# Decayed attention and a two-layer MLP on one core: the prologue's weight steps, mask, first group of w_in and loads in another order

## The chip, the cores and the metric

The kernel runs on one core of one Trainium2 chip. The metric is the device time of one execution in microseconds (us), the median of the runs shown. The core's engines are TensorE (PE; PEld is its weight load), VectorE (DVE), ScalarE (ACT) and GpSimd (POOL); SyncE (SP) issues nearly all DMAs.

## The reference

Attention with a decayed state (batch 4, 8 heads, 768 positions, 64 channels, blocks of 64 positions), then an MLP on its 3072 tokens:

```
for b in range(nb):                      # 12 blocks of 64 positions
    intra = einsum('bhic,bhjc->bhij', qb, kb) * Dmask        # lam**(i-j), causal
    intra = einsum('bhij,bhjd->bhid', intra, vb)
    inter = einsum('bhid,bhde->bhie', qb * lam_pow, kv_state)
    out[:, :, sl] = intra + inter
    kv_state = lam_block * kv_state + einsum('bhsd,bhse->bhde', kb * rev_pow, vb)
h = x @ w_in                             # 3072x512 by 512x2048
g = maximum(h, 0)**2
return g @ w_out                         # 2048x512
```

## The kernel before

**Tiles.** Two blocks of 64 positions (a pair for all heads) are a chunk; chunks 0 to 3 give the tokens of the first group (m = 0, 512 tokens), chunks 4 to 7 those of the second. Every fp32 operand of the MLP is split into an upper part (fp32r, `wh`, `xh`, `gh`) and the rest (`wl`, `xl`, `gl`), and a product is the sum of three: upper by upper, rest by upper, upper by rest. So one column tile f of the hidden layer (`hidden(m, f)`, L638) is 12 products of 128x512, and its share of the output (`project(m, f)`, L674, L675, L679) 12 more.

**Order.** The program is laid out by hand: each engine runs its instructions in the order of the code, so an instruction that waits holds up all that stands behind it on its engine. The same holds for SP's loads.

**Prologue.** `warm(4)` (L79) multiplies zeros on PE. `get_near` makes from lam the near powers (ACT copy L384, DVE copy L385), `get_mask` the decay mask of a block (PE L391: 14 products of 64 by 32 columns; DVE copy L397 of 128x224), `get_qpow` the powers for q. Chunk t: `prep_k` and `prep_q` on POOL (L511, L506), `scores` on PE, `masked` on DVE (L517, the mask times the scores), `news` on PE (what the chunk adds to the states) and `state` on DVE (L546: the old state by the decay `fd`, plus the news, four instructions of 128x64 for each block), `early` on PE (the result), `split` (ACT L618 `xh`, DVE L619 `xl`). `copy_vx` and `copy_qx` (ACT L171, L176) copy halves of v and q to the other partitions.

**Weight units.** A unit u is a piece of both weights that is loaded by SP (`wload`, L227) and split by seven steps: ACT `first_hi` (absolute value, L244), DVE `clamp` (L257), ACT `first_lo` (L249), DVE `shift` (L261), `sign` (L268), `rounded` (L274), ACT `upper` (L285, into `wh`), DVE `lower` (L290, into `wl`). With `shared`, DVE does the first half of `lower` and POOL the second (L293), behind a marker copy of one element (L297, `turn`). Unit 0 is half as wide as the others (128x512 where they have 128x1024). Unit 0 feeds f = 0, unit u the column tiles behind it.

**Loads and gates.** A `gate` is a tiny ACT copy (L135) or DVE memset (L137) that writes into the buffer which a load is about to fill, so that the load waits for the engine's place in its order. In the prologue `gate(V, chunk 4)` stands behind `state(1)`, and `wload(2, nc.scalar)`, which has an ACT gate, behind the second `split`; SP issues unit 2 behind the first two loads of chunk 4.

**Group m = 0.** For f = 0 to 15 the loop runs `hidden(0, f)`, then for unit u = f + 2 the DVE steps `clamp`, `shift`, `sign`, the `upper` and `lower` of unit u - 1, then relu, square and rest of the tile (ACT L645, L649, L654, DVE L659 `gl`), `rounded`, and `project` of the tile before. Between them stand steps of chunks 4 to 7: `look` (scores and news), `masked`, `fade` (ACT L564: four instructions that multiply the state by the decay), `advance` (DVE L342: adds the news to it), `result` and `split`. At f = 0 and at f = 1 and 2 three extra products of 384 or 512 columns stand ahead of the 12 (L634); the first of the 12 writes over what they leave.

Behind m = 0 come a second group of the same kind (m = 1) and a part for the other 2048 tokens in a scheme with fewer products; the change touches neither.

Of the kernel before, what the change touches and what calls it, by code (L numbers as in the profile page):

```python
# [15 lines left out]
P = 128  # L16
B, H, S, D = 4, 8, 768, 64
C = 128
# [23 lines left out]
def body(ctx: ExitStack, tc: tile.TileContext, qT, kT, kvq, lam, w, out):  # L42
# [86 lines left out]
    def load_kf(t):  # L129
        nc.sync.dma_start(out=chunk[t]["kf"], in_=kT[t])  # L130
# [120 lines left out]
    def first(u):  # L251
        first_hi(u)
        first_lo(u)
# [81 lines left out]
    move = wk.tile([L, 2 * L - T], F32, name="move", tag="gh")  # L335
    nc.gpsimd.memset(move, 0.0)
    ones_where(move, L - T, [[-1, 2 * L - T]])
    mask = small.tile([P, 2, 2, L], F32, name="mask")


# [44 lines left out]
        V.tensor_copy(y[L:P], x)  # L385

    def get_mask():
        n = ps_h.tile([P, NB - 1, 4, T], F32, name="h")
        for b in range(NB - 1):
            for y, r in enumerate(rows):  # L390
                nc.tensor.matmul(  # L391
                    n[r, b], move[:, b * T : b * T + L], near[0:L, :, 2 * y : 2 * y + 2],
                    start=True, stop=True, skip_group_check=True,
                )
        for y, r in enumerate(rows):
            nc.scalar.copy(mask[r, :, :, L - T : L], near[r, :, 2 * y : 2 * y + 2])
        V.tensor_copy(mask.rearrange("k j a (b t) -> k b (j a) t", b=NB)[:, 0 : NB - 1], n)  # L397

    blk = wk.tile([H, NPR, L], F32, name="blk", tag="gh")
    nc.gpsimd.tensor_tensor(  # L400
# [7 lines left out]
    def get_qpow():  # L408
        q = two_banks(ps_a, "att")
        a, b = q[:, 0, 0 : NPR * L], q[:, 1, 0:4]  # L410
        nc.tensor.matmul(a, odd, blk.rearrange("h p i -> h (p i)"), start=True, stop=True)
        nc.tensor.matmul(b, half, four, start=True, stop=True)
        nc.scalar.copy(qpow.rearrange("k p i -> k (p i)"), a)
        nc.scalar.copy(fd, b)
# [34 lines left out]
                        )  # L449
        return g.begun  # L450

    def news(t, banks, at, begun=(), keys=range(2)):
# [3 lines left out]
        u_of[t] = [banks[1 - b][:, at : at + NPR * D] for b in range(n)]  # L456
        for a in range(2):
            for j in range(2):
                for y in range(2):
                    for b in range(n):  # L460
# [78 lines left out]
    def state(t):  # L539
        for b, u in enumerate(u_of.pop(t)):  # L540
# [11 lines left out]
            else:  # L552
                nc.scalar.copy(new, u)

    faded = {}

    def fade(t, b):
# [69 lines left out]

    g_of, accs = {}, {}

    def hidden(m, f, xh, xl):  # L630
# [206 lines left out]
    def early_news(t):  # L837
        second = ps_h.tile([P, DM], F32, name="h")
        news(t, [ps_h.tile([P, DM], F32, name="h"), second], 0)

    def first_scores(t, x):
# [6 lines left out]
    first(0)  # L848
    get_near()
    for op in (clamp, shift, sign, rounded):  # L850
        op(0)
    first_scores(0, banks())
    get_qpow()
    get_mask()
    prep_k(0)
    prep_q(0)
    prep_k(1)
    upper(0)
    copy_vx(0)
    masked(0)  # L860
    lower(0)
    early_news(0)
    state(0)
    first_hi(1)
    copy_qx(0)
    first_scores(1, banks())
    prep_q(1)
    copy_vx(1)
    masked(1)
    clamp(1)  # L870
    early_news(1)
    copy_qx(1)
    early(0, two_banks(ps_a, "att"))
    state(1)
    place(4)
    gate(V, chunk[4]["all"])
    first_scores(2, banks())
    low[0] = split(0, o[0])
    prep_k(2)
    prep_q(2)  # L880
    copy_vx(2)
    early_news(2)
    masked(2)
    first_lo(1)
    copy_qx(2)
    low[0]()
    load_part(4, 0)
    load_part(4, 2)
    early(1, banks())
    low[1] = split(1, o[1])  # L890
    wload(2, nc.scalar)
    load_kf(4)
    load_part(4, 1)
    load_vx(4)
    state(2)
    first_scores(3, two_banks(ps_a, "att"))
    place_rest(3)
    prep_k(3)
    prep_q(3)
    prep_k(4)  # L900
    prep_q(4)
    copy_vx(3)
    early_news(3)
    masked(3)
    low[1]()
    copy_qx(3)
    early(2, banks())
    low[2] = split(2, o[2])
    state(3)
    early(3, banks())  # L910
# [12 lines left out]
    lower(1, True)
    first_lo(2)
    opening.close()
# [1 line left out]

    prev = None
    for m in range(PLAIN):
        if m == 0:  # L930
            new_x(1)
        else:
            middle.close()
            ps_b = hidden_part.enter_context(tc.tile_pool(name="ps_b", bufs=1, side="right", space=PSUM))
            held += [
                wk.tile([P, KT, N], F32, name=f"held{k}", tag=n) for k, n in enumerate(("xh", "xl"))
            ]
        for f in range(NF):
            h = hidden(m, f, *xs_of[m])
            if m == 0:  # L940
# [16 lines left out]
                if u_ < NLOT:  # L957
                    if f:
                        clamp(u_)
                    if f == 1:  # L960
                        upper(u_ - 1)
                        lower(u_ - 1)
                    if f:
                        shift(u_)
                    sign(u_)
                if f > 1:
                    upper(u_ - 1)
# [22 lines left out]
                    copy_qx(t)  # L990
                if step == 2:
                    attend(t, o)
                if f == 0:
                    fade(t, 0)
                if u_ + 1 < NLOT:
                    first(u_ + 1)
                if prev is not None:
                    project(*prev)
                if step == 0:
                    look(t)  # L1000
                    if f:
                        fade(t, 0)
                if f >= NF - NPAIR:
                    w_plain(f - (NF - NPAIR))
            else:
# [495 lines left out]
```

## Time and profile before

| what | us |
|---|---|
| median of 3 runs | 566.7 (566.15 to 566.91) |
| the profiled execution | 566.81 |
| its span, first to last instruction | 565.0 |
| mean granted TensorE clock | 0.991 |

| engine | busy us | share of the span | instructions |
|---|---|---|---|
| PE | 555.0 | 98% | 5353 |
| PEld | 461.2 | 82% | 5353 |
| DVE | 438.2 | 78% | 763 |
| ACT | 348.3 | 62% | 617 |
| POOL | 83.0 | 15% | 96 |

All durations below come from the profiled execution, 0.11 us above the median; 1.81 us of its time lie outside its span. A timeline row gives an instruction's start, its duration, engine, line, operation, output and inputs, how many like it follow one another, and in brackets how long the engine was idle ahead of it and what ended the wait. A granted clock of 1.00 is 2.4 GHz, 0.50 is 1.2 GHz. One product on PE often has two records, and records of one engine overlap by some hundredths of a microsecond.

### The profile page before, as it was taken

How to read it: one execution, taken by the hardware profiler on the slowest of the kernel's cores; microseconds unless marked ns; L12 is line 12 of the kernel's file. 1: busy time of each engine (PE TensorE's matmuls, PEld its weight loads, DVE VectorE, ACT ScalarE, POOL GpSimd, SP SyncE). 2: the span in 40 equal slices, each digit the busy share in tenths (PEclk: the TensorE clock that was granted, in tenths of full speed). 3: DMA queues.
4: the chain of work that ended last, by engine and by line, in shares of the span. 5: the costliest groups of instructions: out<-in, count | busy, mean ns of one | idle time of the engine just before them, and what ended most of it. 6: DMA issues, size and time to landing. Idle time of an engine off the chain costs nothing.

```text
span 565.0 us, 13666 instructions
## 1 busy us (share of the span) xinstructions
PE 555.0 (98%) x5353; PEld 461.2 (82%) x5353; DVE 438.2 (78%) x763; ACT 348.3 (62%) x617; POOL 83.0 (15%) x96
## 2 busy tenths in 40 slices
PE   7899999999999999999999999999999999999997
PEld 4777888888888888887888878888888888888887
DVE  6889999967888755755655587877599889989884
ACT  2889988856666666664564687676754453443450
POOL 6523342341322223300000000000000000000000
PEclk8799999999999999999999999999999999999999
DMA  8577669976988865357899988999698999999541
GB/s 330 207 259 243 218 230 278 359 226 229 306 293 280 284 206 150 98 171 206 316 374 380 303 298 247 308 300 309 217 363 295 404 344 346 366 329 348 185 130 56
DMA packets 89407, 152.41 MB, mean 270 GB/s; under 512 B 7680, under 2 KB 34816, under 8 KB 89344
## 3 DMA queue, kind: packets, MB, share of 16 engines
q1 hardware_dynamic: 89344, 151.55, 80.0%
q8 instruction: 42, 0.69, 0.5%
q14 instruction: 21, 0.17, 0.1%
HBM read 113.77 MB, written 37.75 MB: 268 GB/s over the span
## 4 chain that ended last, share of the span: by engine, by line
PE 93%; DVE 3%; ACT 2%; issue 1%; POOL 0%; ACTq 0%; POOLq 0%
PE factor L1162 25%; PE h L815 18%; PE h L638 15%; PE acc L815 7%; PE acc L674 6%; PE acc L675 5%; PE acc L679 5%; PE h L428 4%; PE b L428 2%; PE att L428 2%; PE att L79 1%; PE h L1162 1%; ACT w L1306 1%; DVE w L1127 1%; DVE A L268 0%
## 5 line engine op out<-in xcount | busy, mean ns | idle before, releaser
L1162 PE MATMUL factor<-w 128*128 128x512 f32 (+1 forms) x614 | 109.4, 335 | 0.1
L1162 PEld LDWEIGHTS factor<-w 128*128 128x128 f32 x614 | 94.0, 188 | 13.7 <-DVE w L1127 0.6
L1125 ACT CAST w<-kept 128x1024 fp32r<-128x1024 f32 (+2 forms) x66 | 47.3, 739 | 40.7 <-PE factor L1162 27.7
L638 PE MATMUL h<-xh,w 128*128 128x512 f32 x240 | 60.1, 392 | 0.0
L815 PE MATMUL h<-w,ring 128*128 128x512 f32 x240 | 58.2, 390 | 0.0
L1127 DVE TENSOR_TENSOR w<-kept,w 128x1024 fp32r<-128x1024 f32 (+2 forms) x66 | 52.6, 831 | 5.4 <-ACT w L1125 5.4
L815 PEld LDWEIGHTS h<-w,ring 128*128 128x128 f32 x240 | 44.9, 188 | 9.8 <-DVE temp L342 0.4
L638 PEld LDWEIGHTS h<-xh,w 128*128 128x128 f32 x240 | 44.6, 188 | 10.0 <-DVE w L290 0.4
L342 DVE TENSOR_TENSOR temp<-h,temp 128x512 f32<-128x512 f32 (+1 forms) x36 | 23.6, 660 | 33.1 <-PE h L815 26.1
L659 DVE TENSOR_TENSOR gl<-h,gh 128x512 fp32r<-128x512 f32 x32 | 22.0, 688 | 34.9 <-ACT h L654 31.2
L674 PE MATMUL acc<-w,gh 128*128 128x512 f32 x112 | 45.6, 407 | 0.0
L645 ACT ACTIVATE h<-h 128x512 f32<-128x512 f32 x32 | 18.6, 582 | 41.5 <-PE h L638 41.5
L675 PE MATMUL acc<-w,gh 128*128 128x512 f32 x112 | 43.9, 392 | 0.0
L679 PE MATMUL acc<-w,gl 128*128 128x512 f32 x112 | 43.8, 391 | 0.0
L506 POOL TENSOR_TENSOR qs<-set,qpow 128x512 f32<-128x512 f32 (+1 forms) x21 | 25.0, 1189 | 87.2 <-PE b L428 87.2
L823 ACT ACTIVATE kept<-kept 128x512 f32<-128x512 f32 x42 | 26.3, 627 | 17.9 <-DVE kept L342 17.8
L638 PE MATMUL h<-xl,w 128*128 128x512 f32 x120 | 32.2, 390 | 0.2 <-DVE xl L619 0.2
L815 PE MATMUL h<-w,wz 128*128 128x512 f32 x120 | 29.6, 390 | 0.1
L815 PE MATMUL h<-w 128*128 128x512 f32 x120 | 29.5, 389 | 0.0
L342 DVE TENSOR_TENSOR kept<-acc,temp 128x512 f32<-128x512 f32 x28 | 19.3, 691 | 11.8 <-PE acc L815 10.8
L824 ACT ACTIVATE kept<-kept 128x512 f32<-128x512 f32 x42 | 26.6, 633 | 1.3
L1125 ACT CAST w<-set 128x1024 fp32r<-128x1024 f32 x14 | 14.7, 1050 | 20.1 <-PE factor L1162 11.1
(257 smaller groups left out, 1258.8 us busy)
## 6 DMA issues: line engine op xcount, KB each, us to landing
w<-td SPq DMA_DIRECT2D x86, 256.0 KB, 5.7
ring<-wd SPq DMA_DIRECT2D x56, 256.0 KB, 4.8
raw<-in_w SPq DMA_DIRECT2D x22, 512.0 KB, 5.7
set<-in_kvq SPq DMA_DIRECT2D x16, 512.0 KB, 3.9
wd<-hl SPq DMA_DIRECT2D x16, 512.0 KB, 5.1
gd<-kept SPq DMA_DIRECT2D x16, 512.0 KB, 5.0
w<-wd SPq DMA_DIRECT2D x28, 256.0 KB, 4.0
wz<-wd SPq DMA_DIRECT2D x28, 256.0 KB, 3.5
```

Source lines behind the costliest of these rows:

```text
L342: lambda o, x, y, op=op: V.tensor_tensor(out=o, in0=x, in1=y, op=op)
L428: nc.tensor.matmul(self.banks[row][rows[col], at : at + D], lhsT, rhs, start=key not in self.begun, stop=stop, skip_group_check=True,)
L638: nc.tensor.matmul(h, wt[:, w_in(f), kt * P : (kt + 1) * P], x[:, kt], start=k == 0, stop=k == 11)
L674: nc.tensor.matmul(accs[m][i], gh[:, cs], wh[:, j], start=f == 0, stop=False)
L675: nc.tensor.matmul(accs[m][i], gh[:, cs], wl[:, j], start=False, stop=False)
L679: nc.tensor.matmul(accs[m][i], gl[:, cs], wh[:, j], start=False, stop=end)
L815: nc.tensor.matmul(bank, w[:, kw * HALF + kt * P : kw * HALF + (kt + 1) * P], x_slot(2 * c + kt, kx), start=first and q == 0, stop=q == 5, ...
L823: nc.scalar.activation(r, r, AF.Relu)
L824: nc.scalar.activation(r, r, AF.Square)
L1125: nc.scalar.copy(h, x)
L1127: V.tensor_tensor(out=l, in0=x, in1=h.bitcast(F32), op=ALU.subtract)
L1162: nc.tensor.matmul(o, x, y, start=begin and q < len(banks), stop=end and q >= len(uses) - len(banks), skip_group_check=True,)
```

## The change

- `warm(2)`: two products on zeros in place of four.
- The order of loads: w_in unit 1 is no longer loaded between the chunks, but behind the chunks 0 to 2 and an ACT gate that follows `get_qpow`; chunk 3 is loaded behind an ACT gate that follows `upper(0)`. The copied halves of v of the chunks 0 to 3 come by DMA (`load_vx`, two loads of 64x256 each) and not by ACT.
- `move`, which POOL fills, has 64x896 elements and not 64x120, in another buffer. The mask is made by 7 products of 128 by 64 columns; ACT copies one half of the partitions from PSUM, DVE the other.
- DVE's `clamp`, `shift` and `sign` of unit 0 stand ahead of the copy that ends `get_near`.
- The states that a chunk's first block leads to (chunks 1, 2, 3) and the second of chunk 3 are made by `fade_in_place` (ACT, four instructions) and `advance_in_place` (DVE, one addition of 128x256) and not by four DVE instructions. The news of chunk 3's second block are made behind `look` of f = 0, in an `acc` bank, and added to the state by DVE behind `rounded(2)`; `fade(4, 0)` on ACT reads that state and stands behind `look` too.
- The first column tile of the hidden layer is made in two halves of 256 columns: the 12 products of the first half ahead of `early(3)`, those of the second at f = 0.
- The extra products at f = 0 to 2 are gone.
- `shift(2)` moves from ahead of `lower(1)` to behind it; `early`, `split` and the weight steps of unit 1 stand in another order.

The core of the diff (the new bodies, and the prologue's order in one column):

```diff
-    warm(4)
+    warm(2)
...
+    move = wk.tile([L, (NB - 1) * P], F32, name="move", tag="A")
     wload(0)
     for t in range(4):
         place(t)
+    for t in range(3):
         load_kf(t)
         load_all(t)
-        if t == 1:
-            wload(1)
+    for t in range(3):
+        load_vx(t)
...
+                n[:, b].rearrange("k y a t -> k (y a t)"), move[:, b * P : (b + 1) * P],
+                near[0:L].rearrange("k j (y a) t -> k y j (a t)", y=2),
...
+        nc.scalar.copy(x[rows[0], 0 : NB - 1], n[rows[0], :, 0])
+        V.tensor_copy(x[rows[1], 0 : NB - 1], n[rows[1], :, 1])
...
+    def fade_in_place(t, b):
+        n = 2 * t + b
+        old, new = (before_block(k).rearrange("p a j d -> p (a j) d") for k in (n, n + 1))
+        for g in range(4):
+            nc.scalar.activation(new[:, g], old[:, g], AF.Identity, scale=fd[:, g : g + 1])
+
+    def advance_in_place(t, b):
+        x = before_block(2 * t + b + 1).rearrange("p a j d -> p (a j d)")
+        add(x, u_of[t][b], x)
...
+    def half_group(i, xh, xl):
+        if not opened:
+            opened.append(ps_h.tile([P, N], F32, name="h"))
+        cs = slice(i * N // 2, (i + 1) * N // 2)
...
     def hidden(m, f, xh, xl):
+        if m == f == 0:
+            half_group(1, xh, xl)
+            return opened.pop()
         h = ps_h.tile([P, N], F32, name="h")
-        n = 3 * C if f == 0 else N
-        for _ in range(3 if m == 0 and f < 3 else 0):
-            nc.tensor.matmul(h[:, 0:n], wh[:, 0, 0:P], xh[:, 0, 0:n], start=True, stop=True)
...
+    early(2, banks())
+    fade_in_place(3, 0)
+    copy_qx(3)
+    first_lo(1)
+    first_news(3)
     prep_k(4)
     prep_q(4)
...
+    half_group(0, *xs_of[0])
+    advance_in_place(3, 0)
     low[2] = split(2, o[2])
...
     shift(1)
     wload(3, V)
     sign(1)
+    low[2]()
+    third_chunk = chunk[3]
+    early(3, banks())
+    fade_in_place(3, 1)
+    rounded(1)
+    wload(4)
     low[3] = split(3, o[3])
     low[3]()
...
                 if step == 0:
                     look(t)
-                    if f:
-                        fade(t, 0)
+                    if f == 0:
+                        second_news(G - 1)
+                        advance_in_place(G - 1, 1)
+                        del u_of[G - 1]
+                        new_x(1)
+                    fade(t, 0)
```

On DVE, from the last weight instruction of lam's powers to the first masked scores (L257, L261, L268, ISA are `clamp`, `shift`, `sign`, `rounded` of unit 0; `near` and `mask` are the copies), before:

```order
L370 COPY pz<-s 8x1
L385 COPY near<-h 64x64
L257 TENSOR_SCALAR A<-A 128x512
L261 TENSOR_SCALAR A<-A 128x512
L268 SCALAR_TENSOR_TENSOR A<-raw,A 128x512
L274 ISA A<-raw,A 128x1024
L397 COPY mask<-h 128x7x4x8
L517 TENSOR_TENSOR a<-open,mask 128x512
```

and now:

```order
L373 COPY pz<-s 8x1
L257 TENSOR_SCALAR A<-A 128x512
L261 TENSOR_SCALAR A<-A 128x512
L268 SCALAR_TENSOR_TENSOR A<-raw,A 128x512
L388 COPY near<-h 64x64
L274 ISA A<-raw,A 128x1024
L402 COPY mask<-h 64x7x4x8
L522 TENSOR_TENSOR a<-open,mask 128x512
```

Three steps of unit 0 went ahead of the copy of `near`, and the mask's copy has half the partitions.

On DVE, from `rounded(1)` (ISA on `A`) and the last `xl` to the addition behind `rounded(2)` (ISA on `third`; L290 on `w` is `lower(1)`, L659 or L699 `gl`), before:

```order
L619 TENSOR_TENSOR xl<-open,xh 128x4x128
L274 ISA A<-raw,A 128x2048
L257 TENSOR_SCALAR third<-third 128x1024
L261 TENSOR_SCALAR third<-third 128x1024
L290 TENSOR_TENSOR w<-A,w 128x512
L268 SCALAR_TENSOR_TENSOR third<-set_96,third 128x1024
L659 TENSOR_TENSOR gl<-h,gh 128x512
L274 ISA third<-set_96,third 128x2048
L517 TENSOR_TENSOR a<-att,mask 128x512
L342 TENSOR_TENSOR st<-att,faded 128x256
```

and now:

```order
L274 ISA A<-raw,A 128x2048
L644 TENSOR_TENSOR xl<-open,xh 128x4x128
L257 TENSOR_SCALAR third<-third 128x1024
L290 TENSOR_TENSOR w<-A,w 128x512
L261 TENSOR_SCALAR third<-third 128x1024
L268 SCALAR_TENSOR_TENSOR third<-set_94,third 128x1024
L699 TENSOR_TENSOR gl<-h,gh 128x512
L274 ISA third<-set_94,third 128x2048
L345 TENSOR_TENSOR st<-acc,st 128x256
L522 TENSOR_TENSOR a<-att,mask 128x512
L345 TENSOR_TENSOR st<-att,faded 128x256
```

`rounded(1)` went ahead of the last `xl`; `shift(2)` stands behind the first `lower`, and an addition to `st` behind `rounded(2)`.

On ACT, from `first_hi(2)` (L244 on `third`) to `upper(2)` (L285 out of `third`) and the decays behind it, before:

```order
L244 ACTIVATE third<-set_96 128x1024
L285 CAST w<-A 128x2x512
L249 ACTIVATE set_96<-set_96 128x1024
L645 ACTIVATE h<-h 128x512
L649 ACTIVATE gh<-h 128x512
L654 ACTIVATE h<-h 128x512
L564 ACTIVATE faded<-st,fd 128x64 x4
L244 ACTIVATE A<-raw 128x1024
L249 ACTIVATE raw<-raw 128x1024
L285 CAST w<-third 128x2x512
L564 ACTIVATE faded<-st,fd 128x64 x4
```

and now:

```order
L244 ACTIVATE third<-set_94 128x1024
L285 CAST w<-A 128x2x512
L249 ACTIVATE set_94<-set_94 128x1024
L685 ACTIVATE h<-h 128x512
L689 ACTIVATE gh<-h 128x512
L694 ACTIVATE h<-h 128x512
L244 ACTIVATE A<-raw 128x1024
L249 ACTIVATE raw<-raw 128x1024
L589 ACTIVATE faded<-st,fd 128x64 x4
L285 CAST w<-third 128x2x512
L589 ACTIVATE faded<-st,fd 128x64 x4
```

The first four decays (L564, now L589) went from ahead of the L244 and L249 of unit 3 to right ahead of `upper(2)`.

## Rows read from the trace of the kernel before

**Rows 1.** The chain that ended last, shares of the span, by engine

```profile
PE 93%; DVE 3%; ACT 2%; issue 1%; POOL 0%; ACTq 0%; POOLq 0%
```

**Rows 2.** Windows: stretch, its length, busy us (xrecords) of PE, PEld, DVE, ACT, POOL, PEclk, DMA share, GB/s

```profile
10.60:20.60 10.00, 7.22 (x239) 6.92 (x239) 9.06 (x23) 6.99 (x19) 8.63 (x8) 0.50 0.67 266
...
20.80:36.00 15.20, 12.68 (x344) 10.31 (x338) 13.05 (x31) 11.18 (x22) 5.00 (x5) 1.00 0.82 271
...
36.00:60.00 24.00, 23.96 (x205) 18.83 (x204) 23.13 (x28) 23.61 (x37) 5.56 (x6) 1.00 0.72 237
```

**Rows 3.** Timeline of PE: start us, us, what, xcount [idle before <-releaser]

```profile
1.32 6.55 PE L79 MATMUL att<-st 128*128 128x512 f32 x8 [1.32 <-POOL st L70]
...
10.19 1.15 PE L391 MATMUL h<-near,move 64*64 64x32 f32 x22
...
13.99 1.02 PE L428 MATMUL h<-set 64*64 64x64 f32 x27 [2.33 <-DVE mask L397]
...
25.66 0.40 PE L428 MATMUL open<-raw,st 64*64 64x64 f32 x12 [1.40 <-issue]
...
32.78 0.97 PE L634 MATMUL h<-xh,w 128*128 128x512 f32 x3
...
39.06 0.84 PE L634 MATMUL h<-xh,w 128*128 128x512 f32 x3
```

**Rows 4.** Timeline of ACT, weight steps and decays around 30 us

```profile
28.76 1.15 ACT L244 ACTIVATE third<-set 128x1024 f32<-128x1024 f32 x1 [1.06 <-DMA set<-in_w]
31.11 1.05 ACT L285 CAST w<-A 128x1024 fp32r<-128x1024 f32 x1 [1.20 <-DVE A L274]
...
34.76 1.05 ACT L564 ACTIVATE faded<-st,fd 128x64 f32<-128x64 f32 x4
...
37.79 1.03 ACT L285 CAST w<-third 128x1024 fp32r<-128x1024 f32 x1
```

**Rows 5.** Timeline of DVE, state updates and weight steps, 21 to 44 us

```profile
21.85 0.85 DVE L546 SCALAR_TENSOR_TENSOR st<-st,fd,h 128x64 f32<-128x64 f32 x4
...
29.86 1.22 DVE L274 CUSTOM_DVE_ANT_0 A<-raw,A 128x2048 uint16<-128x2048 uint16 x1
...
32.92 1.22 DVE L268 SCALAR_TENSOR_TENSOR third<-set,third 128x1024 uint32<-128x1024 uint32 x1
34.87 0.69 DVE L659 TENSOR_TENSOR gl<-h,gh 128x512 fp32r<-128x512 f32 x1 [0.73 <-ACT h L654]
...
37.21 0.42 DVE L342 TENSOR_TENSOR st<-att,faded 128x256 f32<-128x256 f32 x1
...
38.85 1.23 DVE L290 TENSOR_TENSOR w<-third,w 128x1024 fp32r<-128x1024 f32 x1 [0.63 <-ACT w L285]
...
43.33 0.69 DVE L659 TENSOR_TENSOR gl<-h,gh 128x512 fp32r<-128x512 f32 x1
```

**Rows 6.** Timeline of DVE, first weight unit and mask, 9 to 14 us

```profile
9.17 0.22 DVE L385 COPY near<-h 64x64 f32<-64x64 f32 x1 [1.92 <-ACT near L384]
...
11.08 1.09 DVE L268 SCALAR_TENSOR_TENSOR A<-raw,A 128x512 uint32<-128x512 uint32 x1
12.21 1.43 DVE L274 CUSTOM_DVE_ANT_0 A<-raw,A 128x1024 uint16<-128x1024 uint16 x1
13.56 0.38 DVE L397 COPY mask<-h 128x224 f32<-128x224 f32 x1
```

**Rows 7.** Timeline of SP's own DMA queue, gated loads

```profile
19.45 0.80 SPq L157 DMA_DIRECT2D set<-in_kvq  x2
23.34 1.36 SPq L227 DMA_DIRECT2D set<-in_w  x2
```

**Rows 8.** Timeline of POOL: a decayed q, the marker copy, POOL's half of lower(1)

```profile
10.74 0.88 POOL L506 TENSOR_TENSOR qs<-set,qpow 128x256 f32<-128x256 f32 x1
...
33.07 1.11 POOL L297 COPY mark<-w 1x1 f32<-1x1 f32 x1 [8.58 <-DVE w L290]
34.14 1.29 POOL L293 TENSOR_TENSOR w<-A,w 128x512 fp32r<-128x512 f32 x1
```

More of the change, by code (lines that the diff above doesn't have):

```diff
@@ L387, in get_mask @@
     def get_mask():
-        n = ps_h.tile([P, NB - 1, 4, T], F32, name="h")
+        n = ps_h.tile([P, NB - 1, 2, 4, T], F32, name="h")
         for b in range(NB - 1):
[L390 to L394, printed above, removed]
+            nc.tensor.matmul(
+                n[:, b].rearrange("k y a t -> k (y a t)"), move[:, b * P : (b + 1) * P],
+                near[0:L].rearrange("k j (y a) t -> k y j (a t)", y=2),
+                start=True, stop=True, skip_group_check=True,
+            )
         for y, r in enumerate(rows):
             nc.scalar.copy(mask[r, :, :, L - T : L], near[r, :, 2 * y : 2 * y + 2])
-        V.tensor_copy(mask.rearrange("k j a (b t) -> k b (j a) t", b=NB)[:, 0 : NB - 1], n)
+        x = mask.rearrange("k j a (b t) -> k b (j a) t", b=NB)
+        nc.scalar.copy(x[rows[0], 0 : NB - 1], n[rows[0], :, 0])
+        V.tensor_copy(x[rows[1], 0 : NB - 1], n[rows[1], :, 1])
     blk = wk.tile([H, NPR, L], F32, name="blk", tag="gh")
@@ L450, in scores, with news @@
         return g.begun
-    def news(t, banks, at, begun=(), keys=range(2)):
+    def news(t, banks, at, begun=(), keys=range(2), only=range(2)):
         g = Group(banks, begun, keys)
@@ L455, in news @@
         n = 2 if t % NCB < NCB - 1 else 1
-        u_of[t] = [banks[1 - b][:, at : at + NPR * D] for b in range(n)]
+        u_of.setdefault(t, []).extend(banks[1 - b][:, at : at + NPR * D] for b in only if b < n)
         for a in range(2):
@@ L459, in news @@
                 for y in range(2):
-                    for b in range(n):
+                    for b in only[0:n]:
                         r, p = rows[1 - b], 2 * y + a
@@ L553, in state, with step_state @@
                 nc.scalar.copy(new, u)
+    def fade_in_place(t, b):
[6 more added lines that the diff above has]
+        add(x, u_of[t][b], x)
+    def step_state(t, b):
+        n = 2 * t + b
+        old, new = (before_block(k).rearrange("p a j d -> p (a j) d") for k in (n, n + 1))
+        u = u_of[t][b].rearrange("p (g d) -> p g d", g=4)
+        for g in range(4):
+            V.scalar_tensor_tensor(
+                out=new[:, g], in0=old[:, g], scalar=fd[:, g : g + 1], in1=u[:, g],
+                op0=ALU.mult, op1=ALU.add,
+            )
     faded = {}
@@ L839, in early_news, with first_news, second_news @@
         news(t, [ps_h.tile([P, DM], F32, name="h"), second], 0)
+    def first_news(t):
+        x = ps_h.tile([P, DM], F32, name="h")
+        news(t, [x, x], 0, only=(0,))
+    def second_news(t):
+        x = ps_acc.tile([P, DM], F32, name="acc")
+        chunk[t] = third_chunk
+        news(t, [x, x], 0, only=(1,))
+        del chunk[t]
     def first_scores(t, x):
@@ L848, in body @@
     first(0)
+    clamp(0)
+    shift(0)
+    sign(0)
     get_near()
-    for op in (clamp, shift, sign, rounded):
-        op(0)
+    rounded(0)
     first_scores(0, banks())
+    prep_k(0)
     get_qpow()
+    prep_q(0)
+    wload(1, nc.scalar)
     get_mask()
-    prep_k(0)
-    prep_q(0)
+    upper(0)
+    place_rest(3)
+    gate(nc.scalar, chunk[3]["all"])
+    load_all(3)
+    load_kf(3)
+    load_vx(3)
     prep_k(1)
-    upper(0)
-    copy_vx(0)
+    prep_q(1)
+    early_news(0)
     masked(0)
[L861 to L864, printed above, removed]
     copy_qx(0)
     first_scores(1, banks())
-    prep_q(1)
-    copy_vx(1)
+    lower(0)
+    nc.scalar.copy(before_block(1).rearrange("p a j d -> p (a j d)"), u_of[0][0])
+    early(0, two_banks(ps_a, "att"))
+    step_state(0, 1)
     masked(1)
-    clamp(1)
[L871 to L874, printed above, removed]
+    prep_k(2)
+    prep_q(2)
+    first_scores(2, banks())
+    early_news(1)
+    fade_in_place(1, 0)
+    copy_qx(1)
+    advance_in_place(1, 0)
+    step_state(1, 1)
+    masked(2)
+    low[0] = split(0, o[0])
+    first_hi(1)
+    low[0]()
+    early(1, banks())
+    prep_k(3)
+    prep_q(3)
+    clamp(1)
+    early_news(2)
+    first_scores(3, two_banks(ps_a, "att"))
+    fade_in_place(2, 0)
+    copy_qx(2)
+    advance_in_place(2, 0)
+    step_state(2, 1)
     place(4)
     gate(V, chunk[4]["all"])
[L877 to L886, printed above, removed]
     load_part(4, 0)
     load_part(4, 2)
-    early(1, banks())
     low[1] = split(1, o[1])
@@ L962, in body @@
                         lower(u_ - 1)
-                    if f:
-                        shift(u_)
+                    shift(u_)
                     sign(u_)
```

40 lines of the change are left out of this document (15 added, 25 removed).

## The prediction

> **What bounds the kernel now.** I read the chain that ended last first: 93% of it is PE [rows 1], so time is gained only where PE waits or does work that can go. The table of windows says where that is [rows 2]: from 36 us on PE is busy 23.96 of 24.00 us, while in 10.60 to 20.60 it has 7.22 of 10.00 at a granted clock of 0.50, and in 20.80 to 36.00 12.68 of 15.20 at 1.00. Behind 36 us DVE is nearly as full (23.13 of 24.00), so PE can start the steady part earlier only if the weight units come earlier too. I therefore read the timelines of ACT and DVE backwards from the second `gl` (43.33), which opens `project(0, 1)` for PE. DVE runs without a pause from `lower(2)` at 38.85 to there, 4.48 us, and `lower(2)` waited 0.63 us for `upper(2)` on ACT [rows 5]. ACT worked without a pause from `upper(1)`, 31.11, to the end of `upper(2)`, 37.79 + 1.03 = 38.82: 7.71 us. `upper(1)` waited 1.20 us for `rounded(1)` on DVE (29.86 + 1.22 = 31.08), and ahead of it ACT had waited 1.06 us for unit 2's load [rows 4, 5]. So the start is set by `rounded(1)`, then ACT's 7.71 us, then DVE's 4.48. All sums are against the profiled 566.81, 0.11 above the median. What the change gains at the second `gl` it keeps, as long as PE itself is there in time.
>
> **The mask and unit 0.** Before, the mask was copied at 13.56 behind `rounded(0)` and ready at 13.94; PE had waited 2.33 us for it [rows 3, 6]. `clamp`, `shift` and `sign` of unit 0 now run in the 1.92 us in which DVE waited for `near` [rows 6]. Each costs at most half of a `sign` of double width, 1.22 / 2 = 0.61 [rows 5], so 1.83 fits, and I cost them at nothing; that cover has 0.1 us to spare, and where POOL gets between them as at 11.08 (1.09 for a `sign` of half width, POOL busy from 10.74 to 11.62 [rows 6, 8]) the near copy slips by some 0.5. Without two of the four warm products (6.55 us for all, 3.3 for two [rows 3]) PE is free for the next products when DVE's last step is, 9.17 - 1.92 = 7.25, and not at 7.87: 0 to 0.6 better, taken as 0 against that slip. `rounded(0)` starts behind `near` at 9.4 and ends at 10.8 if it still costs 1.43. Of the mask's 14 products, two records each, 22 records took 1.15 us [rows 3], so 0.105 a product and 1.47 for all; 7 with twice the columns cost 0.74 to 1.47. I take the upper end, since half of them may already run at the lower clock, and one wait for the powers of q: 12.0. Two copies of at most 0.38 follow, the second writing into the same tile behind the first: 12.8. That is 1.1 us earlier (1.9 at the other end). `move` is larger by 64x776 for POOL to fill, which I cost at nothing, since DVE's and PE's chain to `near` runs until 9.2; if POOL took over 2 us more the mask would wait.
>
> **Decayed states.** Four DVE instructions of 0.85 [rows 5] become four on ACT (1.05 as L564 [rows 4]) and one DVE addition of 0.42. For four blocks DVE saves 4 x 0.43 = 1.7 and ACT takes 4.2, from which eight copies of v go (now DMA). None of it is on the chain named above unless the gates move.
>
> **Loads.** The DVE gate of chunk 4 stood behind `state(1)`; SP issued at 19.45 [rows 7]. It now stands behind the state of chunk 2, which ended at 21.85 + 0.85 = 22.7; 1.1 earlier that is 21.6. SP holds unit 2 behind those two issues (0.80), so it goes out at 21.6 + 0.16 + 0.8 = 22.5 (before 23.34, by its ACT gate). From issue to ACT's use it took 28.76 - 23.34 = 5.42 us, so 27.9. Bounds: 27.3 if the pair of chunk 4, now just ahead, costs nothing and unit 2's second load gains from less traffic behind it; 28.9 if that pair and the later chunk 3 lie in its way for a further microsecond. I take 27.9: `upper(1)` can follow `first_hi(2)`, 1.15, at 29.05.
>
> **`rounded(1)`.** It stood behind `xl` of chunks 2 and 3, `shift(1)` and `sign(1)`. The last `xl` is now behind it, `shift` and `sign` ahead of the `xl` of chunk 2, in time that DVE spent waiting for PE. PE reaches that chunk 1.1 us earlier by the mask even if its 1.40 us stall ("issue", 25.66 [rows 3]) comes again. So `rounded(1)` ends at 27.5 or so, 28.5 with the stall at a worse place, ahead of 29.05. The load, not DVE, sets `upper(1)`: 2.05 us earlier than 31.11.
>
> **From there to `lower(2)`.** The other steps are not moved by all of that. `upper(1)` ends at 30.1, DVE's half of `lower(1)` at 30.7, `shift(2)` (now behind it) at 31.3, `sign(2)` (1.22, and up to 0.3 for POOL's marker copy between) at 32.7. ACT's relu, square and rest end 34.76 - 31.11 = 3.65 behind the start of `upper(1)`, at 32.7; `gl` ends at 33.35. Now two new waits. First, POOL: its marker copy of one element took 1.11 us beside `sign(2)` and its half of `lower(1)`, 1.29, began at 34.14 as that `sign` ended (32.92 + 1.22) [rows 5, 8]; before, DVE then stood idle for 0.73 [rows 5], so POOL's half was over before `rounded(2)`. Now DVE has no such idle time; the half runs from 32.7 to 34.0, and if `rounded(2)`, which reads two operands from SBUF, waits for it, it ends at 35.2, otherwise at 34.55. Second, the four decays of the state into chunk 4 now wait for DVE's addition behind `rounded(2)` (0.42), and `upper(2)` stands behind them on ACT: 35.2 + 0.35 + 1.05 + 1.03 = 37.6 for `lower(2)`, 1.25 earlier than 38.85; without POOL in the way 34.55 + 2.43 = 37.0, 1.9 earlier. Below 29.05 + 7.71 = 36.8 it cannot come. I take 1.4, nearer to the first, by the row at 34.14.
>
> The Trainium skill, page "SBUF — State Buffer", section "Who interferes with whom", says that DVE and GpSimd share one pair of ports as a lock for a whole instruction, and that a DVE instruction with two SBUF inputs contends with a GpSimd one that reads SBUF. The marker copy of 1.11 us that ended with `sign(2)` agrees. By the page the gain is 1.25, without such a lock 1.9.
>
> **Dropped products and halves.** Between 32.78 and 39.06 PE makes 27 products, 0.233 each [rows 3]; so the six extra ones of 512 columns are 1.4 us and the three of 384 some 0.5. Nothing is gained by them on DVE's chain, but PE no longer binds: without them, and with its start some 1.5 earlier, PE is ready for `project(0, 1)` at about 31 + 36 x 0.233 + 1.1 (one result) = 40.5, and the second `gl` comes at 43.33 - 1.4 = 41.9. The halves (24 products of 256 columns for 12 of 512) cost between nothing and 2.8 more; taken as nothing by columns, and 2.5 us of PE were free in that window [rows 2].
>
> The sum: 566.81 - 1.4 = **565.4**.
>
> **The rivals.**
> - *POOL first.* If POOL's half of `lower(1)` starts during `shift(2)`, ahead of `sign(2)`, that `sign` ends at 31.3 + 1.3 + 1.15 = 33.75, `gl` at 34.35, `rounded(2)` at 35.5 and `lower(2)` comes at 37.9: gain 0.9, 565.9. For it: the change puts `shift(2)` between `lower(1)` and `sign(2)`, which gives POOL the time. Against it: before, `sign` won.
> - *The loads are late.* Unit 2 lands as late as before or up to a microsecond later: `upper(1)` at 29.9 to 30.9, gain 0.4 to -0.6, 566.7. For it: the gated pair moves from 19.45 to 21.8 and chunk 3 and unit 1 come late too; against it, SP's queue was idle from 20.3 to 23.3 [rows 7].
> - *Slower: the clock.* It stood at 0.50 for 10 us in which PE was busy 7.22 [rows 2]. With fillers and warm products gone PE may fall to that level around `hidden(0, 1)`. PE has 41.9 - 40.5 = 1.4 us of slack there and loses half of the time at the low clock; the kernel is slower than before once it lasts over 2 x (1.4 + 1.4) = 5.6 us beyond 31 us. With the 10 us of [rows 2] it is 5.0 - 1.4 = 3.6 later than forecast: 569.0. Against it: in 20.80 to 36.00 PE held 1.00 with 2.5 us idle, more than the change takes out.
> - *More.* Load at 27.3, no lock, the mask at 12.0: 2.0 to 2.6, 564.5, if the decays leave DVE free and PE's earlier end of the prologue lets relu follow.
>
> **How the numbers follow.** A measurement of this kernel tells 0.2%, 1.1 us, from no change: faster is below 565.6, slower above 567.8. Forecast (565.0 to 565.8) 0.45, of it 0.33 faster; POOL first 0.18, of it 0.04 faster; late loads 0.14, of it 0.03 slower; clock 0.09, of it 0.07 slower; more 0.14, all faster. Faster 0.51, same 0.39, slower 0.10. The range leaves out most of the clock's case above (0.07), the worst of the loads (0.03) and a tail of the last rival below (0.05): 563.8 to 567.3.
>
> **What would show it.** In the changed profile: mask copy at 12.4 or so and PE's wait ahead of the first news gone; unit 2 used by ACT at 27.9; `upper(1)` right behind it, waiting for no DVE; `rounded(2)` starting when POOL's half ends; decays ahead of `upper(2)` waiting for DVE; second `gl` at 41.9; the granted clock at 1.00 from 21 us on. Wrong, if `upper(1)` still waits for `rounded(1)`, if the gain at the second `gl` is gone by 60 us, or if a window behind 21 us shows 0.50.

## The result: 7 us slower

| kernel | median us | ratio to before, 95% interval |
|---|---|---|
| before | 566.42 (566.07 to 566.91) | |
| changed | 573.45 (573.30 to 573.64) | 1.0124 (1.0106 to 1.0141) |

The forecast was 565.4, the range 563.8 to 567.3. The changed kernel's profiled execution took 573.30 us (span 571.5), 6.49 more than that of the kernel before. Of these, 5.55 are lost by the second `gl` (48.88 against 43.33 [rows 5]) and 0.94 behind it, 0.57 of them in one wait of PE for a `lower` at 120 us.

**PE up to the mask.** Timeline of PE, changed kernel (columns as in [rows 3]; L381, L416, L393 are the products for `near`, `qpow` and the mask):

```profile
1.32 3.78 PE L79 MATMUL att<-st 128*128 128x512 f32 x4 [1.32 <-POOL st L70]
8.13 1.84 PE L381 MATMUL h<-pz 8*64 8x8 f32 x16 [3.04 <-DVE pz L373]
...
10.96 1.22 PE L416 MATMUL att<-blk,pz 8*128 8x256 f32 x2
...
12.33 3.25 PE L393 MATMUL h<-near,move 64*128 64x64 f32 x14
...
16.43 1.02 PE L433 MATMUL h<-set 64*64 64x64 f32 x27 [0.46 <-DVE mask L402]
...
20.14 0.69 PE L433 MATMUL h<-set 64*64 64x64 f32 x30
...
36.39 1.51 PE L433 MATMUL att<-set 64*64 64x64 f32 x64 [3.41 <-DMA raw<-in_w]
...
38.68 2.91 PE L678 MATMUL h<-xh,w 128*128 128x512 f32 x8
```

The 16 records for `near` take 1.84 us. The first `news` (16.43) take 1.02 for 27 records, what they took in [rows 3] at a granted clock of 0.50; the same kind at 20.14 takes 0.69 for 30. So PE ran at the lower level from the products for `near` on (8 to 10 us) to some 20 us. The column of the clock does not say so in this execution. Windows of the changed kernel, one in that stretch and one later:

```profile
13.00:14.00 1.00, 1.00 (x7) 1.00 (x7) 0.00 (x0) 0.36 (x3) 1.00 (x2) 1.00 0.08 27
38.00:39.00 1.00, 1.00 (x16) 0.88 (x14) 1.00 (x1) 0.97 (x3) 1.00 (x1) 0.50 1.04 426
```

It reads 1.00 at 13 us, with 7 PE records in the microsecond, and 0.50 only at 37 to 40. I read the low clock before its first recorded change from the products, not from the column. (In the three later runs with two warm products the column itself shows 0.50 from between 8.2 and 8.9 us on, to 18.5 us at the earliest. And the other three executions of the changed kernel have a mean granted clock of 0.985 to 0.988, the profiled one 0.997: as an estimate, 0.01 of 571.5 us at half the clock is 11 us more of the low level, about what the column lacks.)

**DVE, POOL, ACT and SP.** The rows that answer [rows 4 to 8], in timelines of the changed kernel:

```profile
5.69 0.89 DVE L345 TENSOR_TENSOR s<-s 8x6 f32<-8x6 f32 x1
...
10.25 0.22 DVE L388 COPY near<-h 64x64 f32<-64x64 f32 x1 [0.39 <-ACT near L387]
...
15.98 0.40 DVE L402 COPY mask<-h 64x224 f32<-64x224 f32 x1 [4.79 <-ACT mask L401]
...
26.13 0.06 DVE L137 MEMSET set<- 1x1 f32 x1
...
37.96 2.31 DVE L268 SCALAR_TENSOR_TENSOR third<-set,third 128x1024 uint32<-128x1024 uint32 x1
40.19 0.68 DVE L699 TENSOR_TENSOR gl<-h,gh 128x512 fp32r<-128x512 f32 x1
...
43.46 0.42 DVE L345 TENSOR_TENSOR st<-att,faded 128x256 f32<-128x256 f32 x1 [0.54 <-ACT faded L589]
...
44.40 1.23 DVE L290 TENSOR_TENSOR w<-third,w 128x1024 fp32r<-128x1024 f32 x1
...
48.88 0.68 DVE L699 TENSOR_TENSOR gl<-h,gh 128x512 fp32r<-128x512 f32 x1
```

The first of these rows in the kernel before:

```profile
5.64 0.15 DVE L342 TENSOR_TENSOR s<-s 8x6 f32<-8x6 f32 x1
```

POOL, ACT and SP in the changed kernel:

```profile
5.54 1.04 POOL L313 TENSOR_SCALAR_AFFINE_SELECT move<-move 64x896 f32<-64x896 f32 x1
...
37.92 1.26 POOL L293 TENSOR_TENSOR w<-A,w 128x512 fp32r<-128x512 f32 x1
```

```profile
34.54 1.12 ACT L244 ACTIVATE third<-set 128x1024 f32<-128x1024 f32 x1 [3.80 <-DMA set<-in_w]
35.55 1.04 ACT L285 CAST w<-A 128x1024 fp32r<-128x1024 f32 x1
...
42.36 1.07 ACT L589 ACTIVATE faded<-st,fd 128x64 f32<-128x64 f32 x4 [0.95 <-DVE st L345]
43.34 1.03 ACT L285 CAST w<-third 128x1024 fp32r<-128x1024 f32 x1
```

```profile
26.28 0.81 SPq L157 DMA_DIRECT2D set<-in_kvq  x2
27.27 0.80 SPq L227 DMA_DIRECT2D set<-in_w  x2
```

To be seen: the selection that fills the large `move` (POOL, 5.54 to 6.58) holds an addition of 8x6 on DVE for 0.89 us (0.15 with the small `move`, in the kernel before and in every run below that has it); `near` comes at 10.25 in place of 9.17; the mask is ready at 15.98 + 0.40 = 16.38 (13.94 before); the gate of chunk 4 runs at 26.13, its pair of loads goes out at 26.28 (19.45) and unit 2 at 27.27 (23.34); ACT can use unit 2 only at 34.54 (28.76), after 3.80 us of idle time; `upper(1)` follows it directly at 35.55 (31.11). From `upper(1)` to the second `gl` it takes 13.33 us, before 12.22: `sign(2)` took 2.31 us beside POOL's half of `lower(1)`, and the decays waited for DVE at 42.36.

### The profile page after: what moved, and what is told of

Same layout as the page of the kernel before. It is cut to its first block, busy times and chain, and to the rows that moved or that the text cites. A ratio compares the mean times of both kernels' runs of the same rounds, so it can differ in the third digit from the quotient of the medians.

```text
span 571.5 us, 13649 instructions
## 1 busy us (share of the span) xinstructions
PE 556.5 (97%) x5338; PEld 463.5 (81%) x5338; DVE 438.8 (77%) x751; ACT 349.4 (61%) x628; POOL 85.2 (15%) x96
## 4 chain that ended last, share of the span: by engine, by line
PE 77%; DVE 14%; ACT 4%; DMA 3%; issue 3%; SPq 0%; DVEq 0%; ACTq 0%
PE factor L1222 25%; PE h L855 18%; PE h L678 8%; PE acc L855 7%; PE acc L714 4%; PE h L433 4%; PE acc L719 3%; PE acc L715 3%; PE b L433 2%; DVE A L268 2%; DVE A L274 1%; DVE A L257 1%; DMA raw<-in_w 1%; DMA set<-in_w 1%; DVE gl L699 1%
## 5 line engine op out<-in xcount | busy, mean ns | idle before, releaser
L678 PEld LDWEIGHTS h<-xh,w 128*128 128x128 f32 x232 | 43.6, 191 | 10.7 <-DVE w L290 1.4
L699 DVE TENSOR_TENSOR gl<-h,gh 128x512 fp32r<-128x512 f32 x32 | 22.0, 687 | 33.5 <-ACT h L694 29.7
L678 PE MATMUL h<-xl,w 128*128 128x512 f32 x116 | 31.0, 389 | 0.0
```

Source lines behind the costliest of these rows:

```text
L678: nc.tensor.matmul(h, wt[:, w_in(f), kt * P : (kt + 1) * P], x[:, kt], start=k == 0, stop=k == 11)
L699: V.tensor_tensor(out=gl, in0=r, in1=gh.bitcast(F32), op=ALU.subtract)
```

## Experiments

Theory A: the two missing warm products leave PE at its low clock, and everything up to the mask is late. Theory B: the place of chunk 4's gate delays the loads by itself. Theory C: the dropped fillers let the clock fall later. L is the place of `shift(2)`, M the form of the mask. Each time is a median, with its ratio to the kernel before as measured beside it. A trace is of one execution, whose own time is given where it lies far from the median. "issue" in a row means that the profile shows nothing that the engine waited for.

**Four warm products.** `after_warm4`:

```diff
-    warm(2)
+    warm(4)
```

> The changed kernel with four products on zeros at the start in place of two, nothing else. Theory A (the two missing products keep TensorE at its lower clock until 20 us, so everything up to the mask is late: the mask was ready at 16.38 us against 13.94 before): the mask is ready by 13.5 us, the first gated pair of loads goes out some 3 us earlier than 26.28, and the time falls by 3 to 5 us to 568.5 to 570.5. Theory B (the gate of chunk 4 stands behind a later state and unit 2's load lands late for that reason alone): the loads move by under 1.5 us and the time stays above 572. Theory C (the fillers dropped at f = 0 to 2 let the clock fall at 37 us): the stretch from 37 to 40 us stays at 0.50 and the time at 573.

570.34, ratio 1.0075 (1.0055 to 1.0095; before 566.64): 3.1 us of the 7 come back, as A said; B and C fall as sole causes. The profiled execution is the slowest of its four (572.36, the others 570.20 to 570.37), so its trace holds only 0.9 of the 3.1: the mask is ready at 14.47 (A said 13.5), the pair goes out at 23.98, unit 2 is in use at 33.24 and the second `gl` comes at 47.59, 1.29 earlier than in the changed kernel. PE's timeline:

```profile
8.14 1.06 PE L381 MATMUL h<-pz 8*64 8x8 f32 x16 [0.17 <-DVE pz L373]
...
10.55 3.13 PE L393 MATMUL h<-near,move 64*128 64x64 f32 x14
```

`near` takes 1.06 us (1.09 before), and the mask's products start at 10.55 in place of 12.33. They still take 3.13: here the clock fell at 10.7 us, just behind their start. Where it fell at 11.4 (`w4_gsf_vxcopy` below) they took 2.44, and at 12.9 (`after_warm4_gate`) 1.77.

**Two warm products in the kernel before.** `before_warm2`, the reverse edit:

> The kernel before with two products on zeros in place of four, nothing else. Theory A: the products for near, qpow and the mask take twice as long as in the kernel before, the mask is ready 0.5 to 2 us later than 13.94 and the time is 567.5 to 569. Theories B and C: no change, 566.2 to 566.9.

569.37, ratio 1.0053 (1.0036 to 1.0071): 2.7 us slower from this one line. But not by the way expected: the mask was ready at 13.06, earlier than 13.94, because `near` started 0.5 us earlier, as the prediction had said. The loss is in what follows: the gated pair went out at 19.20 (19.45 before), but unit 2 at 24.81 in place of 23.34, and ACT had it at 32.12 in place of 28.76; the second `gl` came at 45.38. Windows, and PE's timeline:

```profile
20.00:22.00 2.00, 2.00 (x86) 2.00 (x84) 1.50 (x4) 1.94 (x4) 1.27 (x2) 0.50 0.88 266
22.00:24.00 2.00, 0.91 (x44) 0.77 (x40) 1.32 (x7) 1.07 (x3) 1.04 (x2) 0.96 0.04 8
```

```profile
19.09 0.26 PE L428 MATMUL att<-qs,st 64*64 64x64 f32 x1 [0.60 <-issue]
...
23.64 0.38 PE L428 MATMUL open<-rest,A 64*64 64x64 f32 x9 [1.09 <-issue]
```

The low clock begins at 8.5 and ends at 22.2 us, where it ended between 20.6 and 20.8 [rows 2]. That PE's chain is late by the clock alone is not shown: ahead of the second split, behind which unit 2's gate stands, PE also waits 0.60 and 1.09 us for nothing that the profile shows, as much as the 1.47 us by which unit 2 goes out late. The kernel before has one such wait of 1.40 us, behind that point [rows 3]. They may be waits for instructions: a queue of kind "instruction" moves a packet some 2 to 2.6 us ahead of the end of each of PE's three longest here (at 16.5 to 17.0, 21.0 to 21.5 and 25.0 to 25.5 us, for ends at 19.09, 23.64 and 27.52). The other 1.9 us at ACT came between unit 2's issue and its use (7.31 us in place of 5.42). Whether the missing products move those waits, or this execution had them by chance, no run tells.

**The gate.** `after_warm4_gate`, four products and:

```diff
     step_state(1, 1)
+    place(4)
+    gate(V, chunk[4]["all"])
...
     step_state(2, 1)
-    place(4)
-    gate(V, chunk[4]["all"])
```

> The changed kernel with four products on zeros and with the gate of chunk 4 moved back to behind the state of chunk 1. Theory A: as the run with four products alone, within 1 us. Theory B: the gated pair goes out 3 us or more earlier than in that run, unit 2 is in use by ACT at 29 us or earlier, and the time falls by 2 to 4 us below that run.

569.03, ratio 1.0050 (1.0032 to 1.0068). Timelines of SP, ACT and DVE:

```profile
19.65 1.62 SPq L157 DMA_DIRECT2D set<-in_kvq  x2
```

```profile
28.86 1.14 ACT L244 ACTIVATE third<-set 128x1024 f32<-128x1024 f32 x1 [0.88 <-DMA set<-in_w]
```

```profile
32.30 2.33 DVE L268 SCALAR_TENSOR_TENSOR third<-set,third 128x1024 uint32<-128x1024 uint32 x1
...
43.24 0.68 DVE L699 TENSOR_TENSOR gl<-h,gh 128x512 fp32r<-128x512 f32 x1
```

The pair goes out at 19.65, unit 2 is in use at 28.86 and the second `gl` at 43.24 is back where it was before; the median falls by 1.3, less than B said and more than A did, and the intervals of the two runs overlap. `after_gate`, the same with two warm products:

> The changed kernel with two products on zeros as it is, and the gate of chunk 4 moved back to behind the state of chunk 1. If the gate's place costs as much at the lower clock as at the higher, the time falls by 1 to 3 us below 573.45; if only the clock counts, by under 0.5 us.

570.07, 1.0059 (1.0040 to 1.0077; before 566.81): 3.4 us below 573.45, more than expected and clear of noise. So the gate's place costs time as well, and A and B overlap: 3.1 and 3.4 alone, 4.4 together.

**The fillers.** `before_nofill`, the kernel before without its nine extra products:

> The kernel before without the nine extra products at f = 0 to 2, nothing else. Theory C: the granted clock falls below 1.00 somewhere between 28 and 45 us and the time rises by 1 us or more. Theories A and B: PE is not what sets the second rest of g, so 566.0 to 566.9, with the clock at 1.00 from 21 us on.

566.63, 1.0005 (0.9992 to 1.0019): no change in the kernel before, as A and B said.

**`shift(2)`.** `w4_gate_shift`, the gate run with `shift(2)` ahead of `lower(1)` again:

> The changed kernel with four products on zeros, the gate of chunk 4 behind the state of chunk 1, and shift(2) back ahead of lower(1). Theory L (with shift(2) between lower(1) and sign(2) POOL's half of lower(1) gets ahead of sign(2), which took 2.33 us in place of 1.22): sign(2) takes 1.3 us or less, the second rest of g comes 0.6 to 1.2 us earlier than 43.24, and the time falls by as much below the 569.0 of the run with the shift behind. Against it (the decays on ACT that wait for DVE's addition set upper(2) in any case): under 0.3 us.

```profile
32.54 1.22 DVE L268 SCALAR_TENSOR_TENSOR third<-set,third 128x1024 uint32<-128x1024 uint32 x1
...
43.02 0.68 DVE L699 TENSOR_TENSOR gl<-h,gh 128x512 fp32r<-128x512 f32 x1
```

`sign(2)` takes 1.22 and not 2.33, so POOL did get ahead in the changed kernel. The second `gl` moves by 0.2 only, as the case against L said, and the time does not fall: 569.56 (executions from 567.47 to 571.93), 1.0042 (1.0023 to 1.0060). `w4_gate_shift_fill`, with the extra products at f = 1 and 2 put back too:

> The changed kernel with four products on zeros, the gate of chunk 4 behind the state of chunk 1, shift(2) back ahead of lower(1), and the nine extra products of f = 0 to 2 put back (at 512 columns each; in f = 0 the function returns ahead of them, so six run). If the spread of the run without them (567.5 to 571.9) comes from executions in which the clock falls again at 35 us, the spread shrinks below 2 us and the median falls to 567 to 568.5. If it comes from PE's waits for instructions, nothing changes.

567.84 (567.27 to 570.70), 1.0035 (1.0019 to 1.0051; before 566.53). The median falls by 1.7, but the intervals of the two runs overlap, the spread does not shrink as expected, and the profiled execution (570.52, the second slowest of ten) has 0.50 at 34.6 to 38 us and a wait of PE of 1.90 us ("issue"). Whether the fillers are worth something here is not settled; in the kernel before they were not.

**The mask.** `w4_gate_oldmask`, the gate run with the small `move` and the 14 products, and `after_oldmask`, the changed kernel with them:

> The changed kernel with four products on zeros, the gate of chunk 4 behind the state of chunk 1, and the small move tile and the mask of 14 products as before. Theory M (the large move tile holds POOL until 6.58 us and an addition of DVE of 8 by 6 elements, 0.89 in place of 0.15 us, behind it; 14 records of the wide products take 1.8 to 3.1 us in place of 1.5): the near copy is 0.7 us earlier, the mask ready 1 to 2 us earlier than in the run with the wide mask, and the time falls by 0.5 to 1.5 us below 569.0. Against it (unit 2's load and not the mask sets the rest): within 0.3 us of that run.

> The changed kernel with two products on zeros as it is, and the small move tile and the mask of 14 products as before. Theory M: lam's powers end 0.7 us earlier, the mask's products take 2.9 us or less in place of 3.25 and the time falls by 0.7 to 1.5 us below 573.45. Theory A alone: the products cost the same at the lower clock and only the 0.7 us of POOL comes back, 0.3 to 0.8.

569.59, 1.0051 (1.0033 to 1.0069), and 573.36, 1.0117 (1.0094 to 1.0140). The mask was ready 1.9 and 3.4 us earlier, and nothing of it came through: M fails in both. In the first trace PE waited 1.57 us for a half of v at 14.06 and 2.52 us ("issue") at 21.76, and unit 2 was in use at 30.96, 2.1 later than with the wide mask. In the second (575.03, the slowest of its four) unit 2 went out 1.9 us earlier than in the changed kernel and was in use only 0.2 earlier.

**What is left.** Three runs on top of the 567.84: unit 1's load put back between the chunks (`w4_gsf_load1`), the old mask as well (`w4_gsf_load1_oldmask`), and the halves of v copied by ACT (`w4_gsf_vxcopy`, with the late load and wide mask).

> As the run with four products on zeros, the gate, shift(2) and the extra products put back (567.84), and with unit 1's load between the chunks as in the kernel before. If that load's lateness is what is left: the clamp of unit 1 no longer waits, PE's wait of 2.1 us for DVE's state of chunk 2 goes or shrinks by 1 us, and the time falls by 0.7 to 1.5 us to 566.4 to 567.1. If not: within 0.4 us of 567.84.

> As the run before it, with the mask of 14 products and the small move tile as well. If the mask's form still holds something: 0.5 us or more below the run before it, and the mask ready 1.5 to 3 us earlier. If unit 2's load sets the rest in any case: the mask is earlier, the time the same within 0.4 us.

> As the run with four products on zeros, the gate, shift(2) and the extra products put back (567.84), and the halves of v of chunks 0 to 3 copied by ACT as in the kernel before. If the eight DMAs hold back the loads behind them: unit 1 is in use by ACT earlier and the time falls by 0.5 to 1.3 us. If they only moved work off ACT: the same or up to 0.5 us slower.

568.55, 569.01 and 568.30, none better than 567.84, and none clear of it. The timeline of PE in the second shows why the earlier mask gives nothing:

```profile
18.24 0.37 PE L431 MATMUL att<-a,vx 64*64 64x64 f32 x2 [4.58 <-DMA vx<-in_kvq]
```

PE waits 4.58 us for a half of v that comes by DMA. Then all three together (`w4_gsf_load1_oldmask_vxcopy`):

> As the run with the gate, shift, extra products, load of unit 1 and mask of the kernel before (569.01), and the halves of v copied by ACT. PE's wait of 4.6 us for them is gone, the gated pair goes out 3 to 5 us earlier than 23.10, unit 2 is in use by ACT by 29 us, and the time falls by 2 to 3.5 us to 565.5 to 567. If it does not, the decays on ACT are what is left.

566.32, 0.9987 (0.9972 to 1.0003; before 566.61): the rest is back. The pair goes out at 20.01, 3.1 earlier, and unit 2 is in use at 27.90. The copies by ACT give 2.7 us here and gave nothing alone: by the trace above, the wait for v had taken the place of the other two as the last one. The load or the copies put back singly give nothing here, nor did the mask in the gate run; all three give 1.5 us. The copies with only one of the other two were not run. What is still changed in this kernel (the states by ACT and DVE, the halves, the order of the units' steps) costs nothing in sum that this run can tell.

**The parts that the prediction liked, alone.** On the kernel before: `before_unit0` has `clamp`, `shift` and `sign` of unit 0 ahead of `near`; `before_unit1` has `rounded(1)` ahead of the last `xl`; `before_units` has both.

```diff
+    clamp(0)
+    shift(0)
+    sign(0)
     get_near()
-    for op in (clamp, shift, sign, rounded):
-        op(0)
+    rounded(0)
...
     early(3, banks())
+    shift(1)
+    sign(1)
     low[2]()
-    shift(1)
     wload(3, V)
-    sign(1)
     low[3] = split(3, o[3])
+    rounded(1)
     low[3]()
-    rounded(1)
```

> The kernel before with one part of the change alone: clamp, shift and sign of unit 0 ahead of the near copy on DVE. If the mask sets the gates, the mask is ready 1 us or more earlier than 13.94, the gated pair goes out as much earlier than 19.45 and unit 2 lands earlier; the time falls by 0.3 to 1.2 us. If rounded(1) sets upper(1), as in the kernel before, only the part that PE gives to the later xl comes through: 0 to 0.8. If the clock falls at another point (PE's wait for the mask is shorter), the time may go either way by a microsecond.

> The kernel before with another part alone: shift and sign of unit 1 ahead of the xl of chunk 2 on DVE, and rounded(1) ahead of the xl of chunk 3; gates and loads stay. By the prediction's reading of the kernel before, upper(1) then waits for first_hi(2), that is for unit 2's load, and starts at 29.9 in place of 31.11; the second rest of g comes 1.0 to 1.3 us earlier and the time falls by 0.8 to 1.3 us. If something else sets it, under 0.3.

> The kernel before with both of these parts. The sum of the two: 0.8 to 2 us below the kernel before, if the earlier mask brings the gates and unit 2's load forward; otherwise as the second part alone.

566.46, 0.9994 (0.9983 to 1.0005); 566.37, 0.9989 (0.9980 to 0.9998); 565.58, 0.9980 (0.9968 to 0.9991; before 566.53). The first alone gives nothing clear of noise, the second 0.16 us, at the edge of it, both together 0.95 us; that beats both kernels. ACT and DVE of `before_units`:

```profile
28.58 1.12 ACT L244 ACTIVATE third<-set 128x1024 f32<-128x1024 f32 x1 [2.18 <-DMA set<-in_w]
29.61 1.03 ACT L285 CAST w<-A 128x1024 fp32r<-128x1024 f32 x1
```

```profile
31.68 1.22 DVE L268 SCALAR_TENSOR_TENSOR third<-set,third 128x1024 uint32<-128x1024 uint32 x1
...
41.82 0.69 DVE L659 TENSOR_TENSOR gl<-h,gh 128x512 fp32r<-128x512 f32 x1
```

`upper(1)` stands right behind unit 2's load, 1.5 us earlier than 31.11, and the second `gl` 1.5 earlier than 43.33. But an earlier second `gl` need not reach the end. This execution took 566.83, that of the kernel before 566.81, and PE has a wait that it does not have there:

```profile
182.45 0.46 PE L428 MATMUL b<-set 64*64 64x64 f32 x17 [0.99 <-issue]
```

The traces of `before_unit0` (second `gl` at 42.30, execution 566.84, a wait of 0.73 us for DVE at 394 us) and `before_nofill` (42.50, 567.59, 1.15 us at 183 us) show the like. The 0.95 is the difference of the medians.

## Why the prediction was wrong

| step | predicted | measured in the changed kernel |
|---|---|---|
| two warm products less | 0 to 0.6 better ahead of `near`, taken as 0 | 3.1 us slower, in the whole time |
| mask's products | 0.74 to 1.47 | 3.25 |
| `move` on POOL | nothing | `near` held, 0.89 for 0.15 on DVE |
| mask ready | 12.8 | 16.38 |
| gated pair, unit 2 issued | 21.8, 22.5 | 26.28, 27.27 |
| unit 2: issue to use | 5.42 | 7.27 |
| `upper(1)` | 29.05, set by the load | 35.55, set by the load |
| `upper(1)` to `lower(2)` | 8.4; 8.85 if POOL is first | 8.85 |
| `lower(2)` to the second `gl` | 4.48 | 4.48 |
| second `gl` | 41.9 | 48.88 |

**The step that failed first is the warm products.** I priced them by what they occupy (3.3 us of PE ahead of 7.25) and looked for their worth in PE's time alone. Up to the mask their worth is the clock. The row of L79 shows eight records in 6.55 us and hides that they are not alike. The group by line does (shortest, median and longest in ns), of the kernel before and of the changed one:

```profile
L79 PE MATMUL att<-st x8: 593/1061/1220, 1.3 to 7.3; 128*128 128x512 f32 x8
```

```profile
L79 PE MATMUL att<-st x4: 1057/1057/1220, 1.3 to 4.0; 128*128 128x512 f32 x4
```

With eight records the last takes 0.59 us and `near` follows at once at the high level; with four all take about 1.06 or more, 3.04 us without work follow, and `near` takes 1.84. Where `near` started earlier with two products, at 7.34 us (`before_warm2`) and 7.35 (`after_oldmask`), it took 1.06 and 1.10, and PE fell to the low level at 8.5 and 8.2. So the level is not lost at once, but 1.6 us or more earlier than in the runs with four (10.5 us at the earliest). [Rows 2] show the stretch at 0.50, and I had the clock as the rival on the other side, but put it at 31 us, where the fillers go, and gave it 0.07 for slower. It decided at 8 to 20 us: the mask's products start 1.8 us later than with four. The Trainium skill, page "TensorE: Matmul & The Clock Gate", section "What's actually happening", says that the throttled state is the default and that activity releases it. `near` in 1.84 us with two products and in 1.06 with four, both from 8.1 us on, agrees; by that rule the change loses where I counted nothing. That the time is also lost without a later mask (`before_warm2`) I had not seen either; by what way it is lost there stays open.

**The second is the gates.** I named the chain right: the gate behind chunk 2's state, SP holding unit 2 behind the pair, `upper(1)` behind unit 2. But I took only the mask's shift through it and assumed that chunk 2's state would keep its distance from the mask. In the changed kernel the distance grew: 26.13 - 16.38 = 9.75 us from mask to gate, where chunk 2's state had 22.70 - 13.94 = 8.76 [rows 5, 6] and the old gate's loads 19.45 - 13.94 = 5.5. In these 9.75 us DVE waits only once for long, 0.92 us for PE's news, so it is its own order that takes the time; beside POOL's products `lower(0)` took 1.62 us in place of 0.68 and `clamp(1)` 1.47 in place of 0.81. Unit 2 then took 7.27 us from issue to use. Of the 6.5 us by which `upper(1)` came later than forecast, the mask is 3.6, its distance to the gate 1.0 and the time from issue to use 1.9. From 24.72 to 27.27 us as issue time, runs here show 5.8 to 9.0; the pair just ahead of it and the loads behind it share the queues in all of them, but no run isolates which transfer takes the time.

**The third is the last step of the sum**, that what is gained at the second `gl` is kept. In the traces of `before_unit0`, `before_nofill` and `before_units` it came 0.8 to 1.5 us earlier and the execution ended no earlier.

**Right** were the chain named as setting the second `gl`, the load as the bound of `upper(1)`, POOL ahead of `sign(2)` (a rival of 0.18 that came true), the wait of the decays, and the 4.48 us. `before_units` shows the gain that the prediction counted on, 1.5 us at the second `gl`, and 0.95 in the median. Late loads as a rival had the right mechanism and too small a price: 1 us of lateness where 5.8 came. Of the signs of being wrong one came true: a window behind 21 us shows 0.50 (37 to 40.3 us).

**Open.** With the second `gl` at 43.24 and 43.02 two runs were still 2.4 to 2.8 us slower than before in the median, and their executions scatter over 1.6 and 4.5 us. In both profiled executions (568.53 and 568.04, against 566.81) PE waits 1.11 us ("issue") at 184 us, most of what they are slower. Such waits, and stretches at the low clock at 22 to 26 or 34 to 42 us, appear in some runs and not in others. I can't attribute that rest.

## What to carry to other kernels

Price a product that only keeps TensorE busy by what the products behind it take at either clock, not by its own time, and look at the durations of like products, since the clock column may be silent until its first change. Where loads are gated by an engine's place in its order, follow that place through every instruction put ahead of it, and take the time from a load's issue to its use as a range (5.2 to 9.0 us here) and not as the one value of the kernel before. Judge by medians of whole executions where single traces end 1 to 3 us off them. Move one part at a time: two moves of this change, put into the kernel before by themselves, gain 0.95 us, and the whole change loses 7.

## What the runs showed of the hardware

- After two fp32 products of 512 columns and 2 to 3 us without work PE was at the low level from between 8 and 9 us (in the changed kernel 8 to 10) to between 18.5 and 22.2 us in all four kernels of that kind. In the traces with four products it was at the high level at 8 us (`near` in 1.06 to 1.09 us) and to between 10.5 and 17 us, then low for 3.4 to 10.2 us, at another time in each run.
- The column of the clock can be silent ahead of its first change: in the kernel before, the records of the products on zeros go from 1.22 and 1.06 us down to 0.59 for the last, with the column at 1.00 from the start to 10.5 us.
- A one-instruction selection of 64x896 on POOL held a DVE addition of 8x6 elements until it ended, 0.89 us for 0.15.
- A scalar-tensor-tensor of 128x1024 on DVE took 2.31 to 2.33 us where POOL's product of 128x512 had started just ahead of it, and 1.22 where not.
- Unit 2's first load of 512 KB was in use 5.2 to 9.0 us after its issue, depending on the run.
